# k times v on four 64x64 tiles of TensorE, with a list scheduler for all engines

## The chip, the cores and the metric

The kernel runs on one core of one Trainium2 chip. The metric is the device time of one execution in microseconds (us), taken as the median of several executions. A profile is one execution recorded by the hardware profiler; its span is 1.7 to 1.9 us shorter than the time of its execution. Engines are written as the profile writes them: PE is TensorE, PEld its weight loads, DVE is VectorE, ACT is ScalarE, POOL is GpSimd, SP is SyncE, which here only starts transfers.

## The reference

There are eight batches of 576 tokens, with eight heads of 64 columns. Linear attention is followed by a phase-mixing block.

```python
kv  = einsum('bhsd,bhse->bhde', k, v)            # 64x64 for each head, over 576 tokens
out = einsum('bhsd,bhde->bhse', q, kv)           # "raw" in the kernels
x   = out / sqrt(mean(out*out, -1) + 1e-6) * g_norm      # then the heads side by side: 576x512
theta = x @ w_theta
y   = w_tok_r @ (x * cos(theta)) + w_tok_i @ (x * sin(theta))   # mixing over tokens
u   = x + y
return u + maximum(u @ w_ch, 0)
```

k times v is done in float32, everything after it in float16 with float32 sums. 576 is four times 128 and 64 left over. That "tail" of 64 tokens is what much of this case is about.

## The kernel before

Each batch passes through stages: cast q, transpose q, k times v, raw, normalise, transpose x, theta, sines, z, mix, channel. Hand-tuned start times (START, STEPS) order the instructions of all engines. Batch 0 is worked in pairs of heads, so that it can start on the first loads.

Each row (partition) holds four tokens of a head, and the last 64 tokens lie in separate tiles whose rows 64 to 127 are zero.

```python
for hp in range(HP):                                  # a pair of heads
    for (dst, src) in ((qt, q), (kt, k), (vt, v)):
        nc.sync.dma_start(out=dst[:].rearrange("p h j d -> p h (j d)"),
            in_=src[b, pair, 0:SF, :].rearrange("h (p j) d -> p h (j d)", j=NF))
    if hp == 0:                                       # the tails: rows of 256 bytes
        for (dst, src) in ((kl[0:T], k), (vl[0:T], v), (ql[:], q)):
            nc.sync.dma_start(out=dst, in_=src[b, :, SF:S, :].rearrange("h s d -> s h d"))
# ... (cut)
def attention(b, hp):
    # ... five transposes of q, the fifth of the tail
    for j in range(NT):                               # NT = 5
        for r in range(2):                            # two heads: two column tiles of 64
            nc.tensor.matmul(
                kvp[r * D:(r + 1) * D, hp, :],
                ks[hp][:, r, j, :] if j < NF else kl[:, 2 * hp + r, :],
                vs[hp][:, r, j, :] if j < NF else vl[:, 2 * hp + r, :],
                start=(j == 0), stop=(j == NT - 1))
# ... (cut)
def normalise(b, ti, raw, x):                         # cut to its POOL part
    nc.gpsimd.tensor_scalar(out=ss[:], in0=ss[:], scalar1=D * eps, scalar2=None, op0=ALU.add)
    nc.gpsimd.tensor_tensor(out=rt[:], in0=ss[:], in1=mhalf[:], op=ALU.pow)
```

A matmul of k times v thus uses 64 columns of the array (form 128*64 in the trace), and the last of each five works on rows of which half are zero.

## Time and profile before

The time is 245.4 us (244.1 to 245.8), the span of the profile 243.8 us.

The timeline of PE shows one group of k times v in the steady part. The columns are start, duration, engine, line, operation, output and inputs, tile, form and count.

```profile
125.95 0.44 PE L275 MATMUL qTps_0_2080<-ident_79,qcast_77 128*128 128x128 f16 x5
126.32 0.69 PE L286 MATMUL kv_0_2086<-v_0_1660,k_0_1659 128*64 128x64 f32 x16
126.83 0.29 PE L286 MATMUL kv_0_2086<-vl_72,kl_71 128*64 128x64 f32 x4
127.05 0.23 PE L318 MATMUL raw_2_2098<-kvbd_90,qT_0_1639 128*128 128x128 f16 x1
```

A pair of heads takes from 126.32 to 127.05, that is 0.73 us, and there are four such groups in a batch: 2.9 us. The program has ten matmuls in this group, and the trace has twenty MATMUL records (16 and 4).

The wait list of PE (what was waited for: us in all, times, longest) begins with the start of the kernel:

```profile
PE qTps_0_146 L275 <- DVE qcast_75 L262: 7.0, 1, 7.0
PE qTps_0_146 L275 <- DVE qcast_75 L266: 3.6, 1, 3.6
PE xTpp_1_317 L374 <- DVE x_216 L360: 2.7, 1, 2.7
PE y_0_1146 L488 <- DVE z_8_1143 L454: 2.0, 1, 2.0
```

The second line is the tail of q: the first four transposes were done, the fifth waited 3.6 us for the cast of that tail, and the cast 3.8 us for its load (DVE qcast_75 <- DMA ql_108), which comes in 256-byte rows.

The same by stretch (length, busy us and counts of the engines, granted clock, DMA share, GB/s):

```profile
0.00:40.00 40.00, 22.41 (x251) 15.41 (x252) 20.83 (x50) 18.68 (x37) 16.16 (x29) 0.87 1.04 263
40.00:100.00 60.00, 53.77 (x615) 37.88 (x613) 46.26 (x98) 44.91 (x84) 22.04 (x23) 0.94 0.68 195
100.00:200.00 100.00, 99.38 (x1137) 70.83 (x1135) 90.28 (x192) 82.88 (x155) 39.85 (x41) 1.00 0.53 155
```

Busy time hides short waits, since the records of matmuls overlap (above, 16 of k times v, 222 ns each by the page, start within 0.51 us), so I also use a ledger. Each matmul record of PE is charged the time from its start to the next start that it takes at full clock in an undisturbed run of its kind (0.2155 us at 512 columns, 0.1358 at 320, 0.1092 at 256, 0.056 for a 128x128 transpose or product; k times v 0.0365 per record before, 0.0158 after; the half-width records of the tails 0.070 at 256 columns, 0.034 for transposes of u and 0.0408 for raw). What is over is excess: waits, half clock and some of the changes between forms of the array (five transposes of q take 0.37 us when k times v follows, 125.95 to 126.32 us above, where their charge is 0.28 us). Before, the charges sum to 196.5 us, the first instruction comes at 7.0 us, and the excess is 40.3 us.

### The profile page before, as it was taken

How to read it: one execution, taken by the hardware profiler on the slowest of the kernel's cores; microseconds unless marked ns; L12 is line 12 of the kernel's file. 1: busy time of each engine (PE TensorE's matmuls, PEld its weight loads, DVE VectorE, ACT ScalarE, POOL GpSimd, SP SyncE). 2: the span in 40 equal slices, each digit the busy share in tenths (PEclk: the TensorE clock that was granted, in tenths of full speed). 3: DMA queues.
4: the chain of work that ended last, by engine and by line, in shares of the span. 5: the costliest groups of instructions: out<-in, count | busy, mean ns of one | idle time of the engine just before them, and what ended most of it. 6: DMA issues, size and time to landing. Idle time of an engine off the chain costs nothing.

```text
span 243.8 us, 5915 instructions
## 1 busy us (share of the span) xinstructions
PE 213.7 (88%) x2317; PEld 149.1 (61%) x2317; DVE 186.9 (77%) x396; ACT 169.0 (69%) x316; POOL 85.5 (35%) x99
## 2 busy tenths in 40 slices
PE   0293699999965999999999999999999999999992
PEld 0172357766633876667667767776677766656751
DVE  5235667479876779989899789989998899986442
ACT  2154469727986589799868796988798879865121
POOL 3029811036333453443543344433443354410000
PEclk9998589999995999999999999999999999999999
DMA  5999999933999931189519941896112012113123
GB/s 160 242 364 233 302 283 218 300 128 119 243 289 312 286 117 43 46 221 288 188 60 236 329 154 43 234 296 208 44 46 89 23 46 86 43 27 126 56 98 108
DMA packets 46316, 41.04 MB, mean 168 GB/s; under 512 B 15184, under 2 KB 41424, under 8 KB 46288
## 3 DMA queue, kind: packets, MB, share of 16 engines
q1 hardware_dynamic: 45248, 38.81, 54.5%
q0 software_dynamic: 1040, 1.85, 4.3%
q8 instruction: 18, 0.29, 0.5%
q14 instruction: 10, 0.08, 0.1%
HBM read 33.06 MB, written 9.44 MB: 174 GB/s over the span
## 4 chain that ended last, share of the span: by engine, by line
PE 61%; DVE 15%; POOL 9%; ACT 6%; DMA 3%; issue 2%; SPq 1%; POOLq 1%; ACTq 0%; DVEq 0%
DMA ql_108<-in_q_dram 3%; PE kv_0_3044 L286 1%; PE kv_0_2563 L286 1%; PE kv_0_2086 L286 1%; PE kv_0_415 L286 1%; DVE uT_1145 L493 1%; PE ya_526 L464 1%; PE kv_0_1621 L286 1%; PE kv_0_841 L286 1%; POOL rt_p_335 L357 1%; POOL rt_1_1181 L357 1%; ACT tr_8_1133 L447 1%; ACT tr_8_1606 L447 1%; PE th_1_383 L410 1%; DVE uT_3502 L493 1%
## 5 line engine op out<-in xcount | busy, mean ns | idle before, releaser
L275 PEld LDWEIGHTS <-qcast_75 128*128 128x128 f16 x80 | 5.8, 104 | 14.1 <-DVE qcast_75 L262 7.9
L275 PE MATMUL qTps_0_146<-ident_79,qcast_75 128*128 128x128 f16 x5 | 0.9, 303 | 10.6 <-DVE qcast_75 L262 7.0
L275 PEld LDWEIGHTS <-qcast_77 128*128 128x128 f16 x80 | 5.6, 98 | 1.4 <-issue 0.2
L297 ACT COPY qT_0_192<-qTps_0_146 128x576 f16<-128x576 f16 x1 | 0.6, 640 | 7.7 <-PE qTps_0_146 L275 7.7
L374 PEld LDWEIGHTS <-x_216 128*128 128x128 f16 x16 | 1.3, 122 | 7.2 <-DVE x_216 L360 7.2
L353 POOL TENSOR_SCALAR ss_p_243<-ss_p_243 128x8 f32<-128x8 f32 x1 | 0.3, 338 | 14.0 <-DVE ss_p_243 L349 14.0
L353 POOL TENSOR_SCALAR ss_0_726<-ss_0_726 128x8 f32<-128x8 f32 x1 | 0.2, 235 | 10.8 <-DVE ss_0_726 L349 10.8
L266 DVE CAST qcast_75<-ql_108 64x512 f16<-64x512 f32 x1 | 0.4, 418 | 3.8 <-DMA ql_108<-in_q_dram 3.8
L374 PE MATMUL xTpp_1_317<-ident_79,x_216 128*128 128x128 f16 x4 | 0.6, 308 | 2.7 <-DVE x_216 L360 2.7
L410 PEld LDWEIGHTS <-xT_297 128*128 128x128 f16 x16 | 1.6, 116 | 1.9 <-issue 0.8
L521 ACT COPY u_0_3952<-ups_0_3942 128x512 f16<-128x512 f16 x1 | 0.6, 586 | 2.8 <-PE ups_0_3942 L508 2.8
L488 PEld LDWEIGHTS <-z_8_1143 128*128 128x128 f16 x8 | 0.8, 106 | 2.7 <-DVE z_8_1143 L454 2.5
L360 DVE TENSOR_TENSOR x_4_331<-raw_4_322,rt_4_348 128x512 f16<-128x512 f32 x1 | 0.7, 692 | 2.2 <-POOL rt_4_348 L357 2.2
L515 PEld LDWEIGHTS <-uT_3502 128*128 128x128 f16 (+1 forms) x24 | 1.8, 102 | 0.9
L515 PEld LDWEIGHTS <-uT_525 128*128 128x128 f16 (+1 forms) x24 | 1.8, 102 | 0.9
L515 PEld LDWEIGHTS <-uT_2631 128*128 128x128 f16 (+1 forms) x24 | 1.8, 102 | 0.9
L515 PEld LDWEIGHTS <-uT_3836 128*128 128x128 f16 (+1 forms) x24 | 1.8, 102 | 0.9
L515 PEld LDWEIGHTS <-uT_3078 128*128 128x128 f16 (+1 forms) x24 | 1.8, 102 | 0.9
L515 PEld LDWEIGHTS <-uT_2141 128*128 128x128 f16 (+1 forms) x24 | 1.8, 102 | 0.9
L515 PEld LDWEIGHTS <-uT_1688 128*128 128x128 f16 (+1 forms) x24 | 1.8, 102 | 0.9
L515 PEld LDWEIGHTS <-uT_1145 128*128 128x128 f16 (+1 forms) x24 | 1.8, 102 | 0.9
L410 PEld LDWEIGHTS <-xT_1592 128*128 128x128 f16 x16 | 1.4, 98 | 1.5 <-issue 0.2
(1955 smaller groups left out, 969.0 us busy)
## 6 DMA issues: line engine op xcount, KB each, us to landing
wnat_103<-in_moe_w_tok_r_dram POOLq DMA_DIRECT2D x1, 576.0 KB, 10.0
wnat_104<-in_moe_w_tok_i_dram POOLq DMA_DIRECT2D x1, 576.0 KB, 7.9
kl_67<-in_k_dram SPq DMA_DIRECT2D x4, 128.0 KB, 6.5
vl_68<-in_v_dram SPq DMA_DIRECT2D x4, 128.0 KB, 6.7
kl_71<-in_k_dram SPq DMA_DIRECT2D x4, 128.0 KB, 5.9
vl_72<-in_v_dram SPq DMA_DIRECT2D x4, 128.0 KB, 6.2
wch<-in_moe_w_ch_dram POOLq DMA_DIRECT2D x1, 512.0 KB, 9.3
q_0_111<-in_q_dram SPq DMA_DIRECT2D x1, 256.0 KB, 2.8
```

Of the source, the lines that this page charges most:

```text
L275: nc.tensor.matmul(pq[:, j * P:(j + 1) * P], st["qc", b, hp][:, j, pair, :], ident16[:], is_transpose=True, start=(j == 0), stop=(j == NT ...
L286: nc.tensor.matmul(kvp[r * D:(r + 1) * D, hp, :], ks[hp][:, r, j, :] if j < NF else kl[:, 2 * hp + r, :], vs[hp][:, r, j, :] if j < NF els ...
L297: nc.scalar.copy(out=t[:], in_=pq[:, 0:S])
L357: nc.gpsimd.tensor_tensor(out=rt[:], in0=ss[:], in1=mhalf[:], op=ALU.pow)
L360: nc.vector.tensor_tensor(out=(x if n > 1 else x[:].unsqueeze(1)).rearrange("p j (h e) -> p j h e", e=D), in0=raw[:].rearrange("p (j h e) ...
L374: nc.tensor.matmul(px[:, j, :], st["xp", hp][:, j, :], ident16[:], is_transpose=True, start=(j == 0), stop=(j == NF - 1),)
L410: nc.tensor.matmul(th[:], xT[:, kc, :], st["wth", kc], start=(kc == 0), stop=(kc == NK - 1),)
L447: nc.scalar.activation(out=tr[rows, r * n:(r + 1) * n], in_=src[half], func=AFT.Sin, scale=-RAD, bias=bias,)
L464: nc.tensor.matmul(st["ya"][kc // 2][:, kc % 2, :], st["z", b, m][:, kc * P:(kc + 1) * P], wT[m][:, 0:SH], start=(i == 0 and kc % 2 == 0), ...
L488: nc.tensor.matmul(y[:], st["z", b, m][:, kc * P:(kc + 1) * P], wT[m][:, cols], start=(m == 0), stop=(m == 2 * NF),)
L493: nc.vector.scalar_tensor_tensor(out=st["uT", b][:, kc, cols], in0=y[:], scalar=gcol[:], in1=st["xT", b][:, kc, cols], op0=ALU.mult, op1=A ...
L515: nc.tensor.matmul(vp[half], uT[kc], st["wch"][:, kc, r * n:(r + 1) * n], start=(kc == 0), stop=(kc == NK - 1),)
```

## The change

The intent has four parts.

1. Nine tokens lie in each row, since 576 is 64 times 9. Two heads fill 128 partitions, each row of a load is 2304 bytes, and k and v have no tail. A matmul of k times v is then 64 rows by 64 columns, one of four tiles. A batch has two groups of 36 matmuls for four heads each.
2. The tail of q is loaded once per batch and no longer stands ahead of the first transpose; the tail of raw is four matmuls instead of eight.
3. A list scheduler written in the kernel orders the instructions of all engines by estimated durations and wishes (WANT, BASE), instead of the hand-tuned start times.
4. The same scheduler deals the eight PSUM banks that the program uses one by one, instead of fixed pools per purpose.

The full diff replaces nearly the whole file. Its core, cut:

```diff
-            for j in range(NT):
-                for r in range(2):
-                    nc.tensor.matmul(
-                        kvp[r * D:(r + 1) * D, hp, :],
-                        ks[hp][:, r, j, :] if j < NF else kl[:, 2 * hp + r, :],
-                        vs[hp][:, r, j, :] if j < NF else vl[:, 2 * hp + r, :],
-                        start=(j == 0), stop=(j == NT - 1))
+    def load_kv(b, hp, s):
+        t = live["kvs", b, hp, s]
+        nc.sync.dma_start(
+            out=t[:].rearrange("p j d -> p (j d)"),
+            in_=(k, v)[s][b, 2 * hp:2 * hp + 2].rearrange("h (p j) d -> (h p) (j d)", j=JK))   # JK = 9
+    def kv(b, hps, xy):
+        # ... the two banks kvx and kvy
+        for j in range(JK):
+            for r in range(2):
+                rows = slice(r * D, (r + 1) * D)
+                for hp in hps:
+                    c = r ^ (hp % 2)
+                    dot(tiles[r][c * D:(c + 1) * D, (hp // 2) % tiles[r].shape[1], :],
+                        live["kvs", b, hp, 0][rows, j, :], live["kvs", b, hp, 1][rows, j, :],
+                        j == 0, j == JK - 1)
...
-START = [8.0, 29.9, 51.0, 77.0, 103.5, 129.7, 155.5, 181.9]
-STEPS = { ... }
+WANT = { ... }; BASE = [0.0, 7.24, 27.08, 54.97, 97.67, 125.89, 147.38, 152.98]
+def plan(want=WANT, caps=CAPS, slots=SLOTS, switch=SWITCH):
+    # takes, of the operations that are ready on the engine that can start first, the most wanted one;
+    # keeps clocks of the engines, the eight banks, the buffers and the loads under way
```

## The prediction

> **What bounds the kernel now.** TensorE. The page gives PE 88% busy, DVE 77%, ACT 69%, DMA 59%. From 80 to 200 us PE is 97-100% busy, DVE about 90%, at full clock. In the PE timeline the fifth mix product of successive batches starts at 116.4, 141.5, 166.2 and 191.1 us: 24.9 us a batch. Start-to-start times of one batch there: mix 8.6-8.8, theta 4.1, channel 4.0, k times v 2.9, q transposes 1.5, x transposes 1.2-1.5, raw 1.3, u transposes 1.0. Eight batches plus the mixer transposes are about 199 us; the other 45 us are edges: PE idle 17.4 us in the first 30 us (3.6 us of it the tail of q in 256-byte rows, then pairs arriving by DMA, the last k-times-v at 17.4 us, theta at 27.8), 5.5 us idle in 60-80 us, about 17 us at half clock (granted 0.61 in 20-30, 0.83 in 60-80) and the end.
>
> **What changes, costed.**
> - k times v: 40 column-tiled matmuls (80 fp32 records, 32 ns start to start, 64 ns per matmul for two tiles, 128 ns per tile) become 72 on four tiles. If each tile keeps its pace, nine turns x 115-128 ns = 1.05-1.15 us for four heads, 2.2 us a batch for 2.9. [...] five q transposes take 0.37 us before k times v, though four x transposes take 0.23. Two kv groups a batch instead of four drop 0.2-0.3 us more.
> - The tail of raw is four matmuls instead of eight: 0.1 us.
> - PE waits for banks (up to 0.8 us, about 0.3 us a batch) mostly go.
> - DVE: two z products become one 1024-wide (-0.08 us x 4 a batch), the casts stay equal; about 21.5 us a batch, still under PE. ACT gains about 0.5 us.
> - DMA: 256-byte tails of k and v vanish, k and v come in 2304-byte rows; the q tail no longer holds up the first transpose.
>
> **On the critical path.** All the PE part: 1.2 us a batch, pace 23.6 us, some 10 us over eight batches. Start: b0 lands about 4 us sooner, so 4 us. The 60-80 us hole and its half clock: filled with other work, -4 to -7 us. Small waits and end, 2-3 us. Sum -23 us.
>
> **Predicted: 222 us, 8 in 10 between 213 and 231.** Over 2% faster: 0.95; within 2%: 0.03; slower: 0.02.
>
> **What would show it.** The kv group of 36 matmuls takes about 1.1 us start to start; the pace is 23.3-23.8 us a batch with PE above 97%; first theta near 23.5 us; no PE idle over 1 us after 45 us; the granted clock is low only before 35 us; packets fall by over 10,000.
>
> **What would make it wrong.** (1) Four tiles don't overlap beyond today's 32 ns between records: then a group costs 2.3 us, 14 us in all, and the gain nearly halves. (2) [...] the scheduler places k times v of batch 1 in the middle of the first mix; if the loads of batch 1 (held behind the first mixer matrix) land late, PE stalls and the clock falls. (3) DVE, at about 91% of the new pace, becomes the limiter. (4) The fill is DMA-bound by bytes, so the start gains less than 4 us.

The sum of the forecast was -23 us, 245 to 222 us. That each tile keeps its pace was the author's assumption, and 0.2-0.3 us for the two groups fewer his estimate from the two times of transposes beside it (0.37 us for five is 74 ns each, 0.23 us for four is 57). 0.08 us for two z products made one is near what the traces show: 0.33 us from start to start for each of 512 columns before, 0.60 us for one of 1024 after.

## More of the kernel before

From the page of the kernel before: the busy time of each engine, then the busy tenths and the granted PE clock in 40 slices of 6.1 us, then DMA packets and the queue that carries instructions.

```profile
span 243.8 us, 5915 instructions
PE 213.7 (88%) x2317; PEld 149.1 (61%) x2317; DVE 186.9 (77%) x396; ACT 169.0 (69%) x316; POOL 85.5 (35%) x99
...
PE   0293699999965999999999999999999999999992
...
PEclk9998589999995999999999999999999999999999
...
DMA packets 46316, 41.04 MB, mean 168 GB/s; under 512 B 15184, under 2 KB 41424, under 8 KB 46288
...
q8 instruction: 18, 0.29, 0.5%
```

PE is at nine tenths or more in all slices from the fourteenth to the last but one: it bounds the kernel there. What PE does not fill is the first 30 us, the slices at 67 to 79 us, and the end. The clock is low in the fifth and the thirteenth slice (0.50 from 25 to 30 us, 0.67 from 70 to 80 us).

## The result, and the profile after

The changed kernel is correct and takes 234.5 us (233.9 to 235.1), against 245.4 us. The ratio is 0.958 (95% interval 0.954 to 0.963): 4.2% faster. Executions over 1.5% slower than the fastest of the same kernel are left out of the means. A ratio is the mean time of one kernel's runs over that of the other's in the same rounds, so it is not quite the ratio of the medians that are quoted. The prediction was 222 us, with 213 to 231 as its range: the direction was right, and the size was wrong. Of the 23 us it promised, 11 came.

From the page of the changed kernel:

```profile
span 233.3 us, 6802 instructions
PE 206.1 (88%) x2797; PEld 151.1 (65%) x2797; DVE 179.1 (77%) x366; ACT 162.6 (70%) x339; POOL 83.5 (36%) x97
...
PE   1781679999948999599999999999999999999991
...
PEclk9999597999995899999999999999999999999997
...
DMA packets 29523, 41.09 MB, mean 176 GB/s; under 512 B 6580, under 2 KB 16436, under 8 KB 29492
...
q8 instruction: 22, 0.36, 0.7%
```

Packets fell by 16,800 at the same bytes, as predicted. PE still has holes before 100 us (slices of 5.8 us here), and there are 480 more MATMUL records and four more packets on the instruction queue.

The timeline of PE shows where two groups of k times v run in a row undisturbed:

```profile
116.67 0.39 PE L493 MATMUL pq<-ident,qc 128*128 128x128 f16 x4
116.99 0.27 PE L490 MATMUL kvx<-kvs,kvs 64*64 64x64 f32 x2
...
119.27 0.63 PE L490 MATMUL ths<-wth,xTs 128*64 128x256 f16 x8
```

They take 2.28 us, 1.14 us for each group of 36 matmuls. The four tiles do overlap, and at the predicted pace. The same in the middle of the first of two longer runs of them (four groups, batches 2 and 3, from 63.51 to 72.99 us):

```profile
66.80 0.22 PE L490 MATMUL kvx<-kvs,kvs 64*64 64x64 f32 x1
66.85 0.23 PE L490 MATMUL kvy<-kvs,kvs 64*64 64x64 f32 x2
66.86 0.22 PE L490 MATMUL kvx<-kvs,kvs 64*64 64x64 f32 x1
70.87 0.33 PE L490 MATMUL kvx<-kvs,kvs 64*64 64x64 f32 x1 [3.79 <-DMA kvs<-in_k_dram]
```

PE stood still for 4 us between two matmuls of one group. The wait list has it third, and a second stall of this kind fourth, which is at 95.5 us, in the two groups of batch 4:

```profile
PE px L493 <- DVE x L674: 5.6, 3, 2.7
PE pq L493 <- DVE qc L518: 5.2, 1, 5.2
PE kvx L490 <- DMA kvs<-in_k_dram: 3.8, 1, 3.8
PE kvx L490 <- issue: 2.4, 1, 2.4
```

The first is blamed on a load of k, the second on "issue", that is on nothing that the profile sees. By stretch:

```profile
0.00:40.00 40.00, 24.18 (x344) 18.12 (x345) 21.82 (x51) 21.39 (x46) 14.99 (x27) 0.87 0.94 279
40.00:100.00 60.00, 53.71 (x918) 41.09 (x916) 44.61 (x94) 42.48 (x93) 19.61 (x20) 0.94 0.85 266
100.00:200.00 100.00, 99.76 (x1303) 72.74 (x1301) 93.89 (x187) 87.23 (x179) 48.94 (x50) 1.00 0.34 109
```

From 40 to 100 us PE is no busier than before (53.7 of 60 us in both), and the mean clock is the same. From 100 us on it is full. The ledger of PE, in us (worked out from the traces as described above):

```
                                   before  changed  changed again  e_fetch45  h_fetchwarm
charge of k times v                  23.4     18.2           18.2       18.2         18.2
charge of all other matmuls         173.2    172.3          172.3      172.3        179.5
first start, and excess to 40 us     25.3     26.2           25.2       27.0         17.2
excess from 40 to 100 us             11.5     10.2            9.1        2.4          2.3
excess from 100 us to the end        10.5      6.4            6.1        9.2          9.2
span                                243.8    233.3          231.1      229.2        226.4
```

("Changed again" is the run f_after below. h_fetchwarm has 128 idle matmuls in its charges.) Figures are rounded, so a column can miss its span by 0.1. The steady part gave what was predicted: 5.2 us from k times v, 0.9 us from the other matmuls and 4.1 us of small waits after 100 us, where about 10 us was promised. The two other large terms failed: the start, where 4 us was promised, gave nothing, and the hole at 60 to 80 us, which was to be filled, was replaced by another.

### The profile page after: what moved, and what is told of

It is laid out like the page before. It is cut to its first block, busy times and chain, and to the rows that moved or that the text cites. A ratio compares the mean times of both kernels' runs of the same rounds, so it can differ in the third digit from the quotient of the medians.

```text
span 233.3 us, 6802 instructions
## 1 busy us (share of the span) xinstructions
PE 206.1 (88%) x2797; PEld 151.1 (65%) x2797; DVE 179.1 (77%) x366; ACT 162.6 (70%) x339; POOL 83.5 (36%) x97
## 4 chain that ended last, share of the span: by engine, by line
PE 76%; ACT 6%; DVE 5%; POOL 4%; DMA 4%; issue 2%; SPq 1%; DVEq 0%
PE ys L490 25%; PE vps L490 13%; PE ths L490 12%; PE kvx L490 6%; PE pus L493 4%; PE px L493 4%; PE rw L490 3%; POOL rt_p L666 3%; PE kvy L490 3%; PE pq L493 3%; ACT trs L747 2%; DMA kvs<-in_v_dram 2%; PE yas L490 2%; DMA kvs<-in_k_dram 2%; DVE fs L726 1%
## 5 line engine op out<-in xcount | busy, mean ns | idle before, releaser
L490 PE MATMUL ys<-wT,zs 128*128 128x320 f16 (+1 forms) x540 | 73.8, 289 | 0.0
L490 PEld LDWEIGHTS <-zs 128*128 128x128 f16 x576 | 55.6, 99 | 15.5 <-issue 0.9
L666 POOL TENSOR_TENSOR rt<-ss,mhalf 128x8 f32<-128x8 f32 x36 | 61.1, 1697 | 3.0
L490 PE MATMUL ths<-wth,xTs 128*128 128x512 f16 (+1 forms) x192 | 38.3, 355 | 1.3 <-DVE fs L726 1.3
L793 DVE SCALAR_TENSOR_TENSOR uTs<-ys,gcol,xTs 128x320 f16<-128x320 f32 (+1 forms) x60 | 30.4, 512 | 11.7 <-PE ys L490 11.6
L490 PE MATMUL vps<-wch,uTs 128*128 128x512 f16 (+1 forms) x192 | 37.6, 344 | 0.0
L490 PE MATMUL kvx<-kvs,kvs 64*64 64x64 f32 x576 | 25.6, 236 | 8.0 <-DMA kvs<-in_k_dram 3.8
L490 PEld LDWEIGHTS kvx<-kvs,kvs 64*64 64x64 f32 x576 | 23.4, 149 | 8.1 <-DMA qfs<-in_q_dram 3.9
L747 ACT ACTIVATE trs<-fs 128x512 f16<-128x512 f32 (+1 forms) x48 | 26.8, 564 | 2.4 <-DVE fs L726 1.7
L747 ACT ACTIVATE trs<-fas 128x512 f16<-128x512 f32 (+1 forms) x48 | 27.1, 568 | 0.7 <-DVE fas L733 0.3
L674 DVE TENSOR_TENSOR xs<-rw,rt 128x512 f16<-128x512 f32 x36 | 24.6, 684 | 3.8 <-POOL rt L666 3.2
L701 ACT ACTIVATE xTs<-px,gcol 128x512 f16<-128x512 f16 (+1 forms) x36 | 23.3, 650 | 3.7 <-PE px L493 3.5
L490 PE MATMUL kvy<-kvs,kvs 64*64 64x64 f32 x576 | 25.6, 237 | 0.0
L490 PEld LDWEIGHTS kvy<-kvs,kvs 64*64 64x64 f32 x576 | 23.4, 149 | 2.6 <-issue 2.6
L654 DVE TENSOR_REDUCE ss<-sqs 128x8 f32<-128x512 f32 x36 | 23.5, 678 | 1.2 <-ACT sqs L649 0.8
L490 PEld LDWEIGHTS <-xTs 128*128 128x128 f16 (+1 forms) x192 | 15.1, 104 | 13.5 <-issue 2.1
```

The lines of the kernel that those rows point to most:

```text
L490: nc.tensor.matmul(dst, lhsT, rhs, start=first, stop=last)
L654: nc.vector.reduce_sum(out=ss[:], in_=live["sqs", b, ti][:].rearrange("p (h e) -> p h e", h=H), axis=mybir.AxisListType.X,)
L666: nc.gpsimd.tensor_tensor(out=rt[:], in0=st["ss", b, ti][:], in1=mhalf[:], op=ALU.pow)
L674: nc.vector.tensor_tensor(out=x.rearrange("p j (h e) -> p j h e", e=D), in0=live["rw", b, ti][:].rearrange("p (j h e) -> p j h e", j=n, e= ...
L701: nc.scalar.activation(out=live["xTs", b][:, :, cols], in_=live["px", b, 10 + ti][:, :, 0:cols.stop - cols.start], func=AFT.Copy, scale=gc ...
L747: nc.scalar.activation(out=dst, in_=src, func=AFT.Sin, scale=-RAD, bias=math.pi / 2 if cos else 0.0)
```

## The experiments

Two questions are open: what the two stalls are, and why the start gained nothing.

For the stalls there are two theories. D (data): PE waits for something in that place, the late load of k that the wait list names. F (fetch): PE waits for its own instructions. The trace gives a reason to think of F. PE has 5634 instruction records (matmuls, weight loads and 40 of its sequencer), and the instruction queue carried 22 packets of 16 KB: 5634/256 is 22.0. Before, it was 4680 records and 18 packets: 18.3. So a packet is a block of 256 instructions. The trace shows packets on this queue at 68.05 to 69.12 and at 95.56 to 96.62 us, and PE resumes 1.7 and 1.5 us after each. The first can be seen in the DMA view of the changed kernel, in the stretch from 64.9 to 68.0 us and then in that from 68.0 to 69.2 us (packets, MB, share); q8 carries nothing in the first:

```profile
q1 hardware_dynamic: 1057, 0.72, 90.5%
q14 instruction: 1, 0.01, 0.6%
```

```profile
q1 hardware_dynamic: 261, 0.24, 67.3%
q8 instruction: 1, 0.02, 5.5%
```

Counting PE's records from zero in the order of their starts, the stalls come at records 1729 and 2497, which are 6 x 256 + 193 and 9 x 256 + 193. Outside k times v a block lasts 5.7 to 18 us. In a run of k times v, with four records per matmul and 36 matmuls in 1.14 us, it lasts about 2.0 us.

For the start, theory P is that the powers on POOL hold it: five of them, each 1.67 us and 0.25 us for the addition before it, in a row, with 2.4 us of issuing mixer transfers between the first and the second.

The first four kernels ran on one chip together (the kernel before took 244.4 us there).

### a_same: the four-group run without the load of k that it waits for

This kernel gives a wrong result (relative error 0.39). The second half of batch 3 in k times v reads the k and v of the first half, which landed earlier.

```diff
+                    src = hp - 2 if (b, hps[0]) == (3, 2) else hp
-                        live["kvs", b, hp, 0][rows, j, :], live["kvs", b, hp, 1][rows, j, :],
+                        live["kvs", b, src, 0][rows, j, :], live["kvs", b, src, 1][rows, j, :],
```

> Wrong on purpose: in batch 3 the second group of k times v reads the k and v of the first group, which were used 1.1 us earlier, so no late load can hold it; order and number of instructions are unchanged. Theory F (instruction fetch: four k-times-v groups in a row, 576 instructions of which one fp32 matmul makes four, outrun the 256-instruction fetches): the PE stall of 3.9 us near 67 us stays (over 2.5 us), again with an instruction fetch landing 1.5-2 us before PE goes on; time 234-235 us, ratio to before 0.955-0.962. Theory D (the last k of batch 3 lands late, as the wait list says): the stall goes, and with it the half clock after it; 227-229 us, ratio 0.925-0.935.

It took 233.8 us, ratio 0.9585 (0.9546 to 0.9624). Both stalls stay, at the same records 1729 and 2497, and the wait list now names neither a load nor anything else for them:

```profile
PE kvx L490 <- issue: 3.4, 1, 3.4
PE kvy L490 <- issue: 2.8, 1, 2.8
```

The load was not what held PE; D falls for the first stall. The name in the wait list was an inference of the profile from semaphore events.

### b_move3: the four-group run cut into two runs of two

k times v of batch 3 moves to a later place in the order. The result is correct.

```diff
+    move([("kv", 3, 0), ("kv", 3, 1)], ("y", 1, 4))
+    move([("kvc", 3, c) for c in range(4)], ("xT", 2, 0))
+    where["kvx", 3], where["kvy", 3] = ("ps", 0, "kvp"), ("ps", 5, "kvp")
```

> Same results: the two k-times-v groups of batch 3 are moved on TensorE behind the fifth mix product of batch 1, some 6.5 us later, so that the run of four groups becomes two runs of two; everything else keeps its order. Theory F: the stall near 67 us falls from 3.9 us to under 1.5 us and the half clock of 6.8 us after it does not come; 227-230 us, ratio 0.925-0.938; the 2.7 us stall near 95 us (two groups, batch 4) may stay. Theory D gives the same gain, so this run is read together with the one that reads other data. If neither holds, 234 us.

It took 233.6 us, 0.9542 (0.9509 to 0.9574). There is no half clock from 30 us to 228 us, and the first stall shrank to 1.7 us, now at record 1985, 7 x 256 + 193; the second is 1.9 us at record 2497. So the stalls fell by about 3 us, in the places that F names. The time hardly moved from that of a_same, and the 227 to 230 us that I had expected was missed. (One of its four runs, 236.9 us, was slow; the three fast ones took 232.4 to 233.8.) Its start was slow in this profile (3.7 us for the second part of k times v of batch 0, for 2.8 in the changed kernel), and two new waits, 0.8 and 1.6 us, stand where the moved groups had been. The second is for a cast of a result of k times v on ACT:

```profile
68.54 1.14 PE L501 MATMUL ys<-wT,zs 128*128 128x256 f16 x9 [1.57 <-ACT bd L644]
```

Runs of two groups still cross two block ends.

### c_nopow0: no powers in batch 0

This is wrong (error 0.86): in batch 0 the addition and the power on POOL give way to one cheap instruction on DVE.

```diff
+        if b == 0:
+            nc.vector.tensor_scalar(
+                out=rt[:], in0=st["ss", b, ti][:], scalar1=D * eps, scalar2=-0.5, op0=ALU.add, op1=ALU.mult
+            )
+            return
```

> Wrong on purpose: for batch 0 alone the power on GpSimd (five times 0.25 + 1.67 us, one after another, with 2.5 us of DMA issues between the first and the second) is replaced by one small DVE operation that gives other numbers. Theory P (this GpSimd chain sets the first theta at 26.1 us): first theta at 19-21 us, time 3-5 us shorter than the changed kernel, 229-232 us. Theory L (the loads of batch 0 and of the mixers set the start): first theta moves by under 2 us, or the PE only waits for the mixer weights instead, and the time stays within 1.5 us of 234.5.

It took 231.8 us, 0.9487 (0.9460 to 0.9513). The first theta starts at 25.5 us, where P expected 19 to 21 us; in the changed kernel it is at 26.1 us. Without the power chain, DVE is what the x transposes wait for. It stands still for 3.0 us until the squares of the next raw are there:

```profile
19.01 0.69 DVE L654 TENSOR_REDUCE ss_p<-sqs_p 128x8 f32<-128x512 f32 x1 [2.96 <-ACT sqs_p L649]
```

These are late because the second part of k times v of batch 0 ends at 17.9 us, for 16.5 in the changed kernel: its last load landed at 14.1 us for 13.4, and in this profile the clock was half until 16.1 us, for 12.2 (read from the pace of k times v, about 53 ns a record and then 30: the trace of the changed kernel has no record of the clock before 12.2 us, where the page prints full). The sums, the casts of the theta weights (which had landed by 17.6 us) and the x products then follow one another on DVE. So the clock blurs the comparison: kernels with the changed start have the first theta at 25.9 to 26.9 us (a_same, b_move3, f_after), and b_move3, with full clock only from 16.7 us, is the one at 26.9. The time is 2.0 us under that of a_same, within what P expected of it, while the first theta is not. P is true of one link only: take it away, and the next, k times v with the squares and sums behind it, holds the first theta. Both stalls remain (3.6 and 2.5 us).

### d_pool: the mixer transfers not issued between the powers

```diff
+    move([("ldwn", 1), ("ldwl",)], ("pow", 0, "p3"))
```

> Same results: three of the four mixer DMA issues on GpSimd (1.65 us) are moved behind the fourth power of batch 0. Theory P: first theta at 24.4 us instead of 26.1 and 1-2 us off the time (232.5-233.5), unless the second mixer matrix, issued 6 us later, then holds up the mixer transposes. Theory L: same or slower, 234-237 us.

It took 235.4 us, 0.9628 (0.9576 to 0.9679): not faster. The first theta came 0.8 us sooner (25.4 us), and PE waited longer for later loads (1.1 us for one of v at 37 us). Neither change on POOL alone brings the 4 us.

### f_after, e_fetch45, e_fetch55: the scheduler told of the blocks

These three ran together, in five rounds (the kernel before 244.6 us). f_after is the changed kernel again, for comparison. The other two tell the scheduler that two successive block ends of PE must be 4.5 or 5.5 us apart. Then its wishes had to be searched anew, so the order differs in other ways too.

```diff
+FETCH, TURN = 256, 4500.0
+def instructions(o):
+    n = {"kv": 36 if o.key[1] else 18, "y": 9, "wT": 5}.get(o.key[0], 4)
+    return n * (4 if o.key[0] == "kv" else 2) * (2 if o.mode == "C" and o.key[0] != "ut" else 1)
...
+        if o.eng == "PE" and chunk[0] % FETCH + instructions(o) >= FETCH:
+            t = max(t, chunk[1] + TURN)
...
+            if chunk[0] % FETCH + instructions(o) >= FETCH:
+                chunk[1] = t + o.dur
+            chunk[0] += instructions(o)
```

> The changed kernel again, on the same chip as the two versions with the fetch rule, as their control: both stalls at the same two instructions (records 1729 and 2497 of TensorE), 3-4 and 2.3-3 us; ratio to before 0.954-0.963.

> Same results. The scheduler is taught the instruction fetch: it counts TensorE instructions (four for an fp32 matmul, two for the others) and lets no operation cross a 256-instruction boundary sooner than 4.5 us after the boundary before; its wish times were searched again under that rule. Theory F: the two stalls of 3.9 and 2.7 us fall to under 1 us each, no half clock between 40 and 225 us, 226-230 us, ratio 0.925-0.942. If the stalls are not the reason for the missed gain, 233-236 us as the changed kernel.

> Same rule with 5.5 us per 256 instructions: the turnaround of a fetch under full DMA load was 5.6-5.9 us in the stalls seen. Theory F: no PE stall without a wait over 0.5 us after 45 us; 227-231 us (its schedule is some 2 us looser than that of 4.5 us), ratio 0.93-0.945.

f_after took 233.1 us, 0.9523 (0.9485 to 0.9560), with stalls of 3.6 and 2.8 us at records 1729 and 2497 once more. e_fetch45 took 230.8 us, 0.9426 (0.9395 to 0.9456), and e_fetch55 230.9 us, 0.9432 (0.9406 to 0.9458). In both, no stall at a block end is longer than 0.25 us. The time of e_fetch45 is just above the 226 to 230 us expected under F; e_fetch55 is inside its range. (The turnaround that it was planned for, from a block end until PE went on, is 5.9 and 4.6 us at the two stalls of the changed kernel, with the DMA engines busy for 0.92 and 0.62 of that time.) The wait list of e_fetch45 starts so, with no "issue" in it:

```profile
PE pq L582 <- DVE qc L607: 5.1, 1, 5.1
PE px L582 <- DVE x L763: 4.1, 3, 2.1
PE yas L579 <- ACT wT L679: 1.8, 2, 1.5
```

The gain is 2.3 us (230.8 for 233.1), though stalls of 6.4 us went. The ledger shows where the rest is: from 40 to 100 us the excess fell by 6.7 us (9.1 to 2.4), but after 100 us it rose by 3.1 and in the start by 1.8. The order that avoids the stalls waits more elsewhere.

### g_warm and h_fetchwarm: PE kept busy while it waits in the start

114 transposes and 14 plain products of the identity, which nobody reads, are put into the waits of batch 0: ahead of the first q transpose and of the x transposes, and the products ahead of the last theta. They write to a bank that is about to be overwritten. The results are correct. h_fetchwarm is e_fetch45 with the same. The calls of warm, and the loop of the products, are cut here:

```diff
+    WARM = {('qT', 0): 38, ('xTp', 1): 40, ('xTp', 2): 18, ('xTp', 3): 18, ('th', 4): 14}
+    def warm(dst, key, b):
+        for _ in range(WARM.get(key, 0) if b == 0 else 0):
+            turn(dst, ident[:], True, True)
```

> Same results. The changed kernel with 128 small matmuls of the identity more (256 instructions, so that the fetch boundaries stay at the same work), put where TensorE idles before the first transposes, the x transposes of batch 0 and the last theta of batch 0; they write banks that the next real matmul overwrites. Theory H (the start is lost to the half clock: k times v of batch 0 takes 4.9 + 3.0 us there, theta 5-6 us for four tiles): k times v of batch 0 starts at full clock or reaches it by 9 us, theta of four tiles takes 3.5-4 us, the first theta comes 1-2 us sooner, and the time falls by 3-5 us against the changed kernel (ratio 0.933-0.942). Theory L (loads and the GpSimd chain set the start whatever the clock): under 1.5 us, ratio 0.946-0.956. The two fetch stalls of 3.6 and 2.8 us stay in both.

> Same results. Fetch rule of 4.5 us and the 128 matmuls together: if both theories F and H hold the gains add, 226-229 us, ratio 0.923-0.936; if only F holds, 230-231 us, ratio 0.940-0.945.

g_warm took 231.1 us (229.5 to 233.5, the last slow), 0.9415 (0.9382 to 0.9449), and h_fetchwarm 228.6 us (226.9 to 230.0), 0.9326 (0.9290 to 0.9362), with 245.3 us for the kernel before. Against f_after's 0.9523 (from another call, each ratio taken to the kernel before on the same chip), the idle work is worth 1.1% (2.6 us), the fetch-aware order 1.0%, and both together 2.0% (4.8 us): they add. The first of these is the least sure: the changed kernel itself had 0.9582 in its first call, so ratios from different calls can differ by 0.6%. h_fetchwarm is 0.9% under g_warm. The PE clock, in the pages of the changed kernel and of h_fetchwarm:

```profile
PEclk9999597999995899999999999999999999999997
```

```profile
PEclk9999988999999999999999999999999999999999
```

In h_fetchwarm the clock is full from 4.9 to 32.2 us. A pair of heads in the k times v of batch 0 takes 1.08 us (1.93 us for each of the first two pairs in the changed kernel: 36 records 29.9 ns apart, against 53.5), the first four theta products 3.9 us (5.2), and theta starts at 24.0 us (26.1 in the changed kernel, 26.5 in e_fetch45, whose order it has):

```profile
26.12 5.15 PE L490 MATMUL ths<-wth,xTs 128*128 128x512 f16 x16
```

```profile
23.98 3.92 PE L579 MATMUL ths<-wth,xTs 128*128 128x512 f16 x16
```

In g_warm, with nothing but transposes on PE from 1.35 us on (38 of the identity, then those of q), the eight transposes of q at 5.2 us took 0.62 us, for 1.03 in the changed kernel: the clock was full. It fell back to half from 8.0 to 11.4 us (granted 0.50 from 8.1 to 11.3), soon after k times v began at 7.7, and its first theta came at 25.6 us, not the 1 to 2 us sooner that was expected; its theta products took 3.9 us too. Half clock in the start thus costs about 2.5 us of the time, if the idle transposes do nothing but keep the clock up; no run separates that.

Adding 256 instructions of PE gave exactly one more packet on the instruction queue (23). The stalls of g_warm are at records 1985 and 2753: the same matmuls as before, since a whole block was added. That alone fits D too.

### i_shift60 and j_shift160: the block ends moved, the order kept

This is the changed kernel in its own order, with 30 or 80 idle transposes (60 or 160 instructions) early in batch 0 and nothing else. Block ends then fall elsewhere in the later order; the data, the banks and the matmuls around them stay.

```diff
+    WARM = {('qT', 0): 30}                                                # i_shift60
+    WARM = {('qT', 0): 30, ('xTp', 1): 25, ('xTp', 2): 13, ('xTp', 3): 12}  # j_shift160
```

> The changed kernel in its own order, with 30 idle transposes of the identity (60 instructions) put ahead of the first q transpose, where TensorE has nothing to do, and nothing else. Theory F (the stalls are TensorE waiting for the next block of 256 of its own instructions): the blocks end 60 instructions earlier in the kernel's own order. In the run of four groups (576 records and 7 others) the block ends fall at records 126 and 382 of the run instead of 186 and 442, so there is still one stall there, of 3 to 4 us, but 60 records earlier in the run. In the two groups of batch 4 they fall 35 records before the run and at record 221, instead of 25 and 281, so the time between them grows from 2.0 us to over 4 us and that stall shrinks from 2.7 us to under 1 us. Sum of the two 3.5 to 4.5 us. Rival D (something in those places of the order: data, a bank, the load of the DMA queues at that moment): both stalls stay after the same matmuls, with 6 to 6.5 us in all. Time 1 us or so under the changed kernel under F; equal to it under D.

> As i_shift60 with 80 idle transposes (160 instructions), the other 50 in the waits for the first x transposes. Theory F: in the run of four groups the block ends fall at records 26, 282 and 538, so there are two stalls in it, after records 282 and 538, of 3 to 4 us for the first and 2 to 4 us for the second; in the two groups of batch 4 only one block end falls inside (record 121) and the stall there goes (under 0.6 us). Sum 5.5 to 7.5 us, and the time 1.5 to 3.5 us above that of i_shift60, less what a warmer clock at the start gives. Rival D: one stall in each place as before, after the same matmuls, and the time of i_shift60.

i_shift60 took 231.4 us (one of six runs, 233.9 us, slow), 0.9454 (0.9416 to 0.9492), and j_shift160 234.0 us, 0.9560 (0.9528 to 0.9593). Of the four-group run in i_shift60 and then in j_shift160, the timeline has these waits and no others:

```profile
69.53 0.27 PE L490 MATMUL kvy<-kvs,kvs 64*64 64x64 f32 x2 [3.90 <-issue]
```

```profile
68.49 0.33 PE L490 MATMUL kvy<-kvs,kvs 64*64 64x64 f32 x4 [1.52 <-issue]
...
74.68 0.27 PE L490 MATMUL kvx<-kvs,kvs 64*64 64x64 f32 x2 [3.85 <-issue]
```

Counted from the first record of the run, they are at records 382 in i_shift60 and at 282 and 538 in j_shift160, to the record where F had put them; in the changed kernel the one stall is at 442. The second stall, in the two groups of batch 4, is gone in both (2.46 and 2.29 us for the two groups, after 5.0 us). D has no reason for any of this: the same matmuls now wait or do not wait, according to a count of instructions that came about 40 us or more before.

Two sizes missed. The first stall of j_shift160 is 1.5 us, not 3 to 4, since that fetch started 0.8 us after the block end and not 2 to 3.7 us. And a third stall, which F had not foretold, appeared in both at record 961, 0.9 to 1.5 us long (in g_warm too, at the same work), at the end of a block that was already short in the changed kernel (5.7 us). The time between the two kernels is not a clean measure of the stalls, as their starts differ too (first theta at 24.6 and 27.0 us).

## Why the prediction was wrong

**k times v: right.** "If each tile keeps its pace, nine turns x 115-128 ns = 1.05-1.15 us for four heads, 2.2 us a batch for 2.9": a group takes 1.14 us in pairs and 1.21 us alone, and the charge fell from 23.4 to 18.2 us, 0.65 us a batch. The tiles overlap in this trace: 36 matmuls in 1.14 us is 32 ns for each, or 127 ns on each tile with all four overlapping. The first warning of the prediction, that the tiles might not overlap, did not come true.

**Waits in the steady part: right.** "PE waits for banks ... mostly go", and two groups of k times v a batch replace four: the excess after 100 us fell from 10.5 to 6.4 us, and 4.8 us of what is left is the end. With the tail of raw and k times v (0.9 and 5.2 us) that makes 10.2 us, where "some 10 us over eight batches" was said. The charges of PE less the 45 mixer transposes are (190.5 - 2.5)/8 = 23.5 us a batch, with 23.3 to 23.8 predicted, and PE is busy for 99.8 of the 100 us from 100 to 200. How the 4.1 us splits between banks, casts, changes of form and order was not tried.

**The start: the failed step is "b0 lands about 4 us sooner, so 4 us".** The loads did so: the last k or v of batch 0 lands at 13.4 us instead of 17.3. But the last head pair of k times v begins at 15.1 us instead of 17.4, and first theta, "near 23.5 us", came at 26.1 instead of 27.8: of 3.9 us, 2.4 and then 1.7 are left. The start and the excess to 40 us did not fall at all (25.3 us before, 26.2 and 25.2 in the two profiles of the changed kernel). Several things stand between a load that lands and work that is done sooner. First, k times v of batch 0 is dearer than before. It is done pair by pair, so that it can follow the loads, and then only two of the four tiles overlap: 36 records 29.9 ns apart (36.3 in the last pair), 1.08 us a pair at full clock and 1.93 us at half clock, where the kernel before took 0.61 and 1.08 us for its 20 records. Four pairs, two of them at half clock in both kernels, took 6.2 us of PE for 3.4. The prediction costed only the form with four tiles. Then come the powers on POOL, with the squares on ACT and the sums and x products on DVE beside them; c_nopow0 and d_pool show that removing the powers, or the issues between them, brings 0.6 to 0.8 us of first theta, where profiles of the same start differ by up to 1.0. And the first theta products ran at half clock (5.2 us; 3.9 us in h_fetchwarm). The idle work in g_warm and h_fetchwarm, where the theta products took 3.9 us, was worth about 2.5 us of time. What the rest of the start would take was not settled. The fourth warning, that the start would gain less than 4 us, came true, but not for its reason, the bytes of the fill: the loads did land sooner.

**The hole: the failed step is "The 60-80 us hole and its half clock: filled with other work, -4 to -7 us".** The old hole was filled. But the scheduler put k times v of batches 2 and 3 into it in one run, and a run of k times v uses up instructions faster than they come: 256 of them in 2.0 us, while the next block took 3.1 and 4.3 us from the block end to landing and 1.5 to 1.7 us more until PE went on, with the DMA engines busy for 0.85 of the time (40 to 100 us). In all runs, where PE stalled, it went on 3.5 to 6.8 us after it had begun the block that ran out. Two stalls, 3.8 and 2.4 us, and a half clock from 70.2 to 77.0 us that came with the first (3.9 us from start to start; in f_after, with 3.6 us, k times v went on at full pace), took the place of the old hole. The excess fell by 1.3 us instead. The prediction counted matmuls in nanoseconds and never as instructions, though the four records per matmul were in the trace of before. Its second warning had the right effect, but the wrong batch and the wrong cause: PE did stall in k times v and the clock did fall, but in batches 3 and 4, not 1, and not for late loads. In the kernel before, groups of 40 records stood alone, blocks lasted 8.5 to 20 us, and no such stall exists.

That the stalls are fetches is shown (a_same, b_move3, e_fetch45, e_fetch55, i_shift60, j_shift160). Each of the 22 fetches of the changed kernel starts between 1.9 us before PE begins a block and 3.2 us after. Why it takes 4.6 and 5.9 us here from a block end until PE goes on, and hardly shows at 140 us, where a block lasted 2.6 us and PE did not stop, is only argued: the DMA engines are busy for 0.30 of the time there (138 to 143 us) and 0.89 around the first stall (64 to 71 us), and the packet for the block end at 142.7 us started at 138.3, before the block end at 140.0.

**Small waits and the end: counted twice.** "Small waits and end, 2-3 us": the small waits are those of the steady part above. The excess of the end itself is 5.1 us before (from 230 us) and 4.8 us after (from 220 us).

**The sum.** Promised: 10 + 4 + 4 to 7 + 2 to 3, about 23 us. In the ledger, to be held against the 10.5 us by which the span fell: 10.2 from the steady part (which holds the end), 1.3 from the hole, minus 0.9 in the start, that is 10.6 with rounding. The range of 213 to 231 us took the good case for the start and the hole together, and its upper end left no room for both to fail.

**A version that beats both.** h_fetchwarm, with a correct result, takes 228.6 us: 6.7% under the kernel before, and about 2% under the changed one.

## What to carry to other kernels

When a change splits work into many small matmuls, count the instructions as well as the time: here a run used up 256 in 2.0 us and stalled PE for 2.4 and 3.8 us, as it went on only 4.6 and 5.9 us after it had begun them, and the profile blamed "issue" once and a load of k once. To test for it, add a few idle instructions far ahead, and see if the stall moves to another matmul. Loads that land sooner helped only as far as the next link of the chain and the clock followed (3.9 us at the loads of batch 0, 1.7 at the first theta), so predict the start link by link.
